# Half of the value weights by a transposing DMA, in a two-layer attention and feed-forward kernel

## The chip, the cores and the metric

The kernel runs on one core of one Trainium2 chip. The time is what the device takes for one execution, in microseconds (us); a run's figure comes from one such execution, and several runs are given by their median. The engines are called PE (TensorE: matmuls; PEld is its loading of weights), DVE (VectorE), ACT (ScalarE), POOL (GpSimd) and SP (SyncE, which here only issues DMAs). Line numbers such as L164 are lines of the kernel; many operations go through a helper, so that they share one line and are told apart by the tiles they read and write.

## The reference, cut to what matters

Four steps, with two functions used twice, on x of 2048 rows and 448 columns:

```
x = x + A(layernorm(x)); x = x + B(layernorm(x)); x = x + A(layernorm(x)); x = x + B(layernorm(x))

A: segments of 32 rows, one after the other, with 8 memory rows ahead of each
   h = concat(mem, segment)
   q, k, v = h @ Wq, h @ Wk, h @ Wv          # 16 heads of 256; each weight is 448 x 16 x 256
   p = softmax(q @ k.T * scale, masked)
   o = sum over heads of (p @ v) @ Wo[head]   # Wo: 16 x 256 x 448
   mem = o[:8]; output = o[8:]
B: h = relu(x @ W_gate) * (x @ W_up); output = h @ W_down     # 448 x 1792, 448 x 1792, 1792 x 448
```

All inputs are bf16.

## The kernel before

The weights of A enter only as products of two of them, so the kernel works these out first, once. For each head it makes `A_sb`, Wq times the transposed Wk (448 x 448 a head), and `B_sb`, Wv times Wo (448 x 448 a head). The main part, which takes most of the time, then runs over the 64 segments of both layers with these products, with the feed-forward blocks in between. The change is in the preparation alone.

The preparation goes by positions of two heads each (512 columns of a weight matrix); there are 8 (`NP`). In its first loop, position p of the query and key weights makes `A_sb`: products named `aps`, `mxw` and `apl`. In its second loop, position p of the value weights makes `B_sb`: products named `bps`, with `wo`, the rows of Wo for these heads. I call the first the query-key stage and the second the value stage; a position of the first is also called a pair, of Wq and Wk.

A product on TensorE sums over the partitions, so the products need each weight with the head's columns on the partitions, while a row of the DRAM tensor holds 4096 columns. So the kernel loads a block as it lies (`load_nat`, L345 on: 384 of 448 rows, as three blocks of 128, into one of six buffers `nat`), and turns it on TensorE by products with an identity (`flip`: six turns into a bank of PSUM called `tpw`, then one copy on DVE or ACT to `qk` or `vT`). The last 64 of the 448 rows are loaded apart, for two blocks at a time into the two halves of the partitions of one of three buffers `natl` (`load_last`), and turned by `flip_last` (four turns into `tpl`, one copy). For the query and key weights the two blocks are Wq and Wk of one position; for the value weights they are two neighbouring positions, and the copy goes to `v3`, which keeps all eight.

`ask(p)` issues the loads of a position, two positions ahead of its use; `queue(p)` and `queue_v(p)` return the tile that a position's products will read, and a list of pieces of work (the flips). The loops take one piece after each product of the position before, so that the flips of position p + 1 stand between the products of position p. Which of DVE and ACT copies a bank is decided when the program is written, by a small plan of how long each is taken (`one_of`); which bank a product takes is decided in the same way (`bank`).

The order of matmuls on TensorE is fixed (`in_order`). The order of the loads on SP is not: a scheduler puts the instructions of an engine in an order by when they could start, so a load that waits for no buffer can move ahead of others that do. A load waits for the buffer's last reader, and also for the DMA eight places before it, because eight completion semaphores are used in turn. `load_wo` issues the loads of `wo` on POOL's queue, each held back until TensorE has come to that place (`spread`); `next_piece` does so on SP for the up weights.

Position 1 of the value stage is followed by the layernorm of the first rows (`normed(row_stats(xp[1]))`: statistics on DVE, a power on POOL, the result `xn` on DVE), and position 2 by their turn on TensorE (`first_rows`).

The main part uses transposing DMAs already: `hk`, `PT` and `xT` are written to DRAM and read back turned, all on SP.

Of the kernel before, what the change touches and what calls it, by code (L numbers as in the profile page):

```python
# [8 lines left out]
BF = mybir.dt.bfloat16  # L9
# [6 lines left out]
DM = 448  # L16
H = 16
NP = 8
# [45 lines left out]
def build_kernel(ctx, tc, A_x, A_mem0, A_Wq, A_Wk, A_Wv, A_Wo, B_W_gate, B_W_up, B_W_down, out,  # L64
                 ntiles=16, nseg=64):
    nc = tc.nc
    P = nc.NUM_PARTITIONS
# [6 lines left out]
    Wv = A_Wv.rearrange("d h e -> d (h e)")  # L74
# [66 lines left out]
    def bank(shape, dtype, name, after=700, hold=False):  # L141

        i = min((i for i in range(8) if i not in held), key=lambda i: free_at[i])
        t = psum.tile(shape, dtype, tag=f"b{i}", name=name)
        bank_of[t.name] = (i, after)
        free_at[i] = now[0] + 1000
        if hold:
            held.add(i)
        return t
# [13 lines left out]
    def mm(out, lhsT, rhs, **k):  # L163
        in_order(nc.tensor.matmul(out, lhsT, rhs, **k))  # L164
        n = 1
        for d in out.shape[1:]:
            n *= d
        pair = lhsT.shape[0] <= 64 or lhsT.shape[-1] == 64 and out.shape[0] == 64
        passed(out, max(25, n / 2.4 + 2.5) * (0.5 if pair else 1))

    def tr(out, src, idn):
        in_order(nc.tensor.transpose(out, src, idn))  # L172
        passed(out, 56)
# [15 lines left out]
    pre = prepare.enter_context(tc.tile_pool(name="pre", bufs=6))  # L189
# [3 lines left out]
    def rows3(src, cols):  # L193
        return src[0:384, cols].rearrange("(k p) n -> p k n", p=P)
# [140 lines left out]
    with prepare:  # L335
# [9 lines left out]
        def load_nat(src, p):  # L345
            t = nats[nn[0] % 6]
            nn[0] += 1
            nc.sync.dma_start(t[:], rows3(src, slice(512 * p, 512 * p + 512)))
            return t

        def load_last(parts):
            t = nats3[n3[0] % 3]
            n3[0] += 1
            for r, (src, p) in zip(FR, parts):
                nc.sync.dma_start(t[r, :], src[384:448, 512 * p:512 * p + 512])
            return t

        asked = {0: (nats[0:2], nats3[0])}

        def ask(p):  # L360

            if p < NP:
                asked[p] = ([load_nat(src, p) for src in (Wq, Wk)], load_last(((Wq, p), (Wk, p))))
            elif p < 2 * NP:
                asked[p] = (load_nat(Wv, p - NP),
                            load_last(((Wv, p - NP), (Wv, p - NP + 1))) if p % 2 == 0 else None)

        def ask_second():

# [7 lines left out]
                    asked[1] = (nats[2:4], load_last(((Wq, 1), (Wk, 1))))  # L377
            nn[0] = 4

        v3 = pre.tile([P, NP, 4, 64], BF, name="v3", bufs=1)  # L380
        until = {dve: 0.0, act: 0.0}

        def one_of(n, per):
# [6 lines left out]
        def share(dst, src, n, per):  # L390
            evac(one_of(n, per), dst, src)

        def flip(nat, e2, dst):
            tp = bank([P, 2, 512], BF, "tpw")
            for kd in range(3):
                for e in range(2):
                    tr(tp[:, e, kd * 128:(kd + 1) * 128],
                       nat[:, kd, (2 * e2 + e) * 128:(2 * e2 + e + 1) * 128], ident[:])
            share(dst, tp[:, :, 0:384], 768, (0.6, 0.82))

        def flip_last(nat, dst):
            tp = bank([P, 4, 128], BF, "tpl")
            for e in range(4):
                tr(tp[:, e, :], nat[:, e * 128:e * 128 + 128], ident[:])
            share(dst, tp[:].rearrange("p e (i d) -> p e i d", i=2), 512, (0.6, 0.82))

        def queue(p):
            if p < NP:
                nat, last = asked[p]
                qk = pre.tile([P, 4, 2, DM], BF, tag="qk", name="qk", bufs=2)  # L410
                us = [lambda i=i, e2=e2: flip(nat[i], e2, qk[:, 2 * e2:2 * e2 + 2, i, 0:384])
                      for e2 in range(2) for i in range(2)]
                us.insert(2, lambda: flip_last(last, qk[:, :, :, 384:DM]))
                return qk, us
            return queue_v(p - NP)

        def queue_v(p):
            us = []
            nat, last = asked[p + NP]
            if p % 2 == 0:  # L420
                us.append(lambda: flip_last(last, v3[:, p:p + 2].rearrange("p a e d -> p e a d")))
            vT = pre.tile([P, 4, 384], BF, tag="vT", name="vT", bufs=2)
            return vT, us + [lambda e2=e2: flip(nat, e2, vT[:, 2 * e2:2 * e2 + 2, :]) for e2 in range(2)]

        def first_rows(xn0):
# [20 lines left out]
        def by_heads(ps, a, b, n):  # L446
            for t in range(2):
                for eo in range(2):
                    mm(ps[FR[eo], 0:n], a(2 * eo + t), b(2 * eo + t), start=(t == 0), stop=(t == 1),
                       tile_position=(0, 64 * eo))  # L450
# [15 lines left out]
        for p in range(NP):  # L466
            hf, p4 = divmod(p, 4)
            qk = ready
            ask(p + 2)
            ready, us = queue(p + 1)  # L470
            todo += us
# [26 lines left out]
        def last_out(p, wo):  # L498

            ps = bank([P, 512], F32, "bps")  # L500
            by_heads(ps, lambda e: v3[:, p, e, :], lambda e: wo[:, e, :], DM)
            hf, p4 = divmod(p, 4)
            share(B_sb[:, hf, 24 + p4, 0:DM], ps[:, 0:DM], DM, (1.28, 0.85))

        for p in range(NP):
            hf, p4 = divmod(p, 4)
            vT = ready
            ask(p + 2 + NP)
            ready, todo = queue_v(p + 1) if p + 1 < NP else (None, [])
            wo = wos.pop(0)  # L510
            if p % 2:
                last_out(p, wo)
            for eo in range(2):
                for kd in range(3):
                    bps = bank([P, 512], F32, "bps")
                    for t in range(2):
                        e = 2 * eo + t
                        mm(bps[:, 0:DM], vT[:, e, kd * 128:(kd + 1) * 128], wo[:, e, :],
                           start=(t == 0), stop=(t == 1))
                    share(B_sb[:, hf, tidx(kd, eo, p4), 0:DM], bps[:, 0:DM], DM, (1.28, 0.85))  # L520
                    if kd < 2 and todo:
                        todo.pop(0)()
            if p % 2 == 0:
                last_out(p, wo)
            if p == 1:
                xn0 = normed(row_stats(xp[1]))
            if p == 2:
                first_rows(xn0)
            if p + 3 < NP:
                load_wo(p + 3)  # L530
            if p >= 3:
                next_piece()
                next_piece()
# [196 lines left out]
    def project_early(hf, chains, hb, j, pairs=(0, 1), head=0, after=700):  # L730

        n = L * len(chains)
        pre = {}
        for pair in [EARLY[i] for i in pairs]:
            for i0 in pair:
                pre[i0] = bank([P, 512], F32, "prj", 700 if i0 else after, hold=True)
            for i in range(head):
                tile_of(pre[pair[0]], hf, pair[0] + i, i, chains, hb, j, range(3), i == 0, False)
            for i in range(6):
                for i0, rows in zip(pair, (slice(0, 64), slice(64, 128))):  # L740
                    mm(pre[i0][:, i * n:(i + 1) * n], A_sb[rows, 3, hf, a_tile(i0 + i), :], moving(hb, j, 3, chains, rows),
                       start=(i == 0 and (head == 0 or i0 != pair[0])), stop=False, skip_group_check=True)
        return pre
# [97 lines left out]
    def active(g):  # L841
        return [c for c in (0, 1) if 0 <= g - c * LAG < nseg]
# [364 lines left out]
    pre, late = project_early(0, active(0), hTb[0], 0), None  # L1207
    for g in range(nsteps):
# [6 lines left out]
        if g % 2 and 0 <= i < nblk + LAG // BLK - 1:  # L1215
            fed = Feed(i)
            pre, late = step(g, fed, pre, late)
        else:
            pre, late = step(g, None, pre, late)
# [27 lines left out]
@with_exitstack  # L1247
def kernel(
    ctx: ExitStack,
    tc: tile.TileContext,  # L1250
    A_x: bass.AP,
    A_mem0: bass.AP,
    A_Wq: bass.AP,
    A_Wk: bass.AP,
    A_Wv: bass.AP,
    A_Wo: bass.AP,
    A_seg_len: bass.AP,
    B_x: bass.AP,
    B_W_gate: bass.AP,
    B_W_up: bass.AP,  # L1260
    B_W_down: bass.AP,
    out: bass.AP,
):
    S = A_x.shape[1]
    ntiles = S // 128
    build_kernel(ctx, tc, A_x, A_mem0, A_Wq, A_Wk, A_Wv, A_Wo, B_W_gate, B_W_up, B_W_down, out,
                 ntiles=ntiles, nseg=4 * ntiles)
# [35 lines left out]
```

## Time and profile before

| | |
|---|---|
| median of 3 runs | 1534.79 us (1534.61 to 1541.23) |
| the profiled execution, its own time | 1534.4 us |
| its span in the profile | 1532.6 us |
| granted TensorE clock | 1.0 |
| query-key stage | to about 42.1 us |
| value stage | 42.1 to 70.7 us |
| main part | from 70.7 us |
| matmuls | 40395 |

The span is the time between the first and last recorded event; the execution's own time is 1.8 us longer. The page of the profile gives the busy time of each engine, the same in 40 slices of 38.3 us, the chain of work that ended last, and groups of instructions. The trace behind it can be asked for stretches of time (busy time of each engine, share of the 16 DMA engines that was busy, and rate), for the instructions of one tile, for an engine's instructions in order, and for how long a DMA took from its issue to its landing. The busy time of TensorE counts matmuls whose ends are modelled; it is not the same as work at full rate.

### The profile page before, as it was taken

The numbers are of one execution on the slowest core, as the hardware profiler recorded it, in microseconds if no ns is written. First come the engines' busy times: TensorE is split into PE (matmuls) and PEld (weight loads), VectorE is DVE, ScalarE is ACT, GpSimd is POOL, SyncE is SP. The second block draws the span as 40 slices with busy tenths as digits, with TensorE's granted clock in tenths as the row PEclk, the third lists the DMA queues.
The fourth block names the chain that finished last, engine by engine and source line by source line (L and its number), as shares of the span: only waits on it lengthen the run. The fifth ranks groups of instructions, "written<-read, shape, count | busy, mean of one in ns | idle before, by whom it ended". The sixth has DMA issues, their size and how long they took to land.

```text
span 1532.6 us, 88890 instructions
## 1 busy us (share of the span) xinstructions
PE 1519.7 (99%) x40395; PEld 1410.9 (92%) x40395; DVE 1079.3 (70%) x3595; ACT 727.9 (47%) x1999; POOL 66.7 (4%) x169
## 2 busy tenths in 40 slices
PE   9999999999999999999999999999999999999998
PEld 6689999999999999999999999999999999999997
DVE  7766777777767677776677777776777777677765
ACT  6744444454444444544444445444444444444444
POOL 3300000000000000000000000000000000000000
PEclk9999999999999999999999999999999999999999
DMA  8620111111111111111111111111111111111100
GB/s 255 204 69 21 31 38 40 30 35 36 34 33 33 40 37 32 36 36 38 31 33 40 37 31 36 36 36 29 37 40 36 31 37 36 32 29 37 30 7 9
DMA packets 148873, 66.96 MB, mean 44 GB/s; under 512 B 108488, under 2 KB 147600, under 8 KB 148496
## 3 DMA queue, kind: packets, MB, share of 16 engines
q1 hardware_dynamic: 114688, 49.22, 12.5%
q10 hardware_dynamic: 32720, 8.38, 2.9%
q8 instruction: 316, 5.18, 1.4%
q0 software_dynamic: 1088, 3.68, 0.7%
q14 instruction: 61, 0.50, 0.1%
HBM read 23.18 MB, written 19.46 MB: 28 GB/s over the span
## 4 chain that ended last, share of the span: by engine, by line
PE 96%; DMA 2%; DVE 2%; issue 0%; POOL 0%; ACT 0%; POOLq 0%; DVEq 0%
PE prj L164 31%; PE ox L164 25%; PE gps L164 6%; PE ups L164 6%; PE dps L164 6%; PE o L164 5%; PE y L164 4%; PE Sx L164 3%; PE bps L164 1%; PE Sm L164 1%; PE ya L164 1%; PE yb L164 1%; PE tpw L172 1%; PE aps L164 1%; DMA xT<-dxn 1%; PE pps L172 1%
## 5 line engine op out<-in xcount | busy, mean ns | idle before, releaser
L164 PE MATMUL prj<-hT,A_sb 128*128 128x80 bf16 (+3 forms) x15232 | 540.3, 199 | 0.4 <-ACT hT L106 0.4
L164 PEld LDWEIGHTS <-A_sb 128*128 128x128 bf16 (+1 forms) x15232 | 500.8, 99 | 20.3 <-issue 0.7
L164 PEld LDWEIGHTS <-B_sb 128*128 128x128 bf16 (+1 forms) x15008 | 484.6, 103 | 15.3 <-issue 2.3
L164 PE MATMUL ox<-Y,B_sb 128*128 128x80 bf16 (+2 forms) x11256 | 436.1, 200 | 2.0 <-issue 2.0
L106 ACT CAST TQ<-prj 128x480 bf16<-128x480 f32 (+1 forms) x380 | 184.8, 498 | 94.8 <-PE prj L164 81.3
L106 ACT CAST Y<-y 128x128 bf16<-128x128 f32 (+2 forms) x452 | 150.3, 411 | 108.3 <-PE y L164 102.6
L106 DVE CAST Y<-y 128x256 bf16<-128x256 f32 (+2 forms) x316 | 135.5, 479 | 39.9 <-PE y L164 39.3
L106 ACT ACTIVATE se<-se 128x160 f32<-128x160 f32 (+2 forms) x270 | 82.0, 304 | 150.2 <-DVE se L106 141.7
L106 DVE CAST TQ<-prj 128x480 bf16<-128x480 f32 (+1 forms) x228 | 125.9, 572 | 8.0 <-PE prj L164 7.6
L164 PE MATMUL gps<-xT,Wg_sb 128*128 128x128 bf16 (+3 forms) x1904 | 128.7, 215 | 0.1
L106 DVE SCALAR_TENSOR_TENSOR hh<-gps,ut 128x512 bf16<-128x512 f32 (+2 forms) x136 | 78.1, 595 | 61.9 <-PE gps L164 39.8
L164 PEld LDWEIGHTS <-Wu_sb 128*128 128x128 bf16 (+1 forms) x1904 | 105.1, 97 | 5.7 <-issue 0.2
L164 PE MATMUL ups<-xT,Wu_sb 128*128 128x128 bf16 (+3 forms) x1632 | 107.0, 216 | 2.6 <-DMA xT<-dxn 2.1
L164 PEld LDWEIGHTS <-Wg_sb 128*128 128x128 bf16 (+1 forms) x1904 | 106.8, 97 | 2.7 <-issue 2.4
L164 PEld LDWEIGHTS <-hk 40*128 40x128 bf16 (+1 forms) x1950 | 99.1, 96 | 8.1 <-issue 0.4
L106 ACT CAST TZ<-prj 64x320 bf16<-64x320 f32 (+2 forms) x264 | 96.8, 377 | 18.8 <-DVE TZ L106 15.9
L106 ACT CAST ut<-ups 128x512 bf16<-128x512 f32 (+1 forms) x102 | 57.5, 564 | 82.1 <-PE ups L164 82.1
L106 ACT COPY os<-o 64x16 f32<-64x16 f32 (+3 forms) x134 | 25.7, 192 | 146.2 <-PE o L164 144.5
L106 DVE TENSOR_REDUCE ssum<-se 128x4 f32<-128x160 f32 (+2 forms) x270 | 73.2, 271 | 30.3 <-ACT se L106 26.5
L164 PE MATMUL dps<-Wd_sb,hh 128*128 128x448 bf16 (+1 forms) x504 | 93.3, 342 | 0.8 <-DVE hh L106 0.8
L106 DVE CAST Y<-ya 128x256 bf16<-128x256 f32 x134 | 56.9, 425 | 47.0 <-PE ya L164 46.5
L164 PEld LDWEIGHTS <-TQ 128*128 128x128 bf16 x1938 | 85.7, 96 | 1.3 <-ACT TQ L106 0.9
(141 smaller groups left out, 1726.2 us busy)
## 6 DMA issues: line engine op xcount, KB each, us to landing
dh<-hT ACTq DMA_DIRECT2D x60, 128.0 KB, 2.2
dx<-PX SPq DMA_DIRECT2D x90, 64.0 KB, 1.6
dxn<-xn SPq DMA_DIRECT2D x29, 128.0 KB, 2.6
wo<-in_A_Wo_dram POOLq DMA_DIRECT2D x8, 448.0 KB, 4.8
nat<-in_A_Wv_dram SPq DMA_DIRECT2D x8, 384.0 KB, 4.4
nat<-in_A_Wq_dram SPq DMA_DIRECT2D x6, 384.0 KB, 4.3
nat<-in_A_Wk_dram SPq DMA_DIRECT2D x6, 384.0 KB, 4.9
xa<-in_A_x_dram SPq DMA_DIRECT2D x32, 56.0 KB, 2.6
```

The source lines that it names most:

```text
L106: r = f(*a, **k)
L164: in_order(nc.tensor.matmul(out, lhsT, rhs, **k))
L172: in_order(nc.tensor.transpose(out, src, idn))
```

## The change

Of the eight value positions, those with an odd number are no longer loaded as they lie and turned on TensorE. One transposing DMA on SP reads all 448 rows of the position's 512 columns and writes them turned, 128 x 4 x 448, into a tile `vTd` with two buffers. The products of such a position read `vTd`, including the last 64 rows, which no longer come from `v3`. Even positions go on as before, but the tail loads of two neighbouring even positions now share a buffer, `v3` holds four positions, and `vT` has one buffer.

```diff
             elif p < 2 * NP:
-                asked[p] = (load_nat(Wv, p - NP),
-                            load_last(((Wv, p - NP), (Wv, p - NP + 1))) if p % 2 == 0 else None)
+                v = p - NP
+                if v % 2:
+                    vT = pre.tile([P, 4, DM], BF, tag="vTd", name="vTd", bufs=2)
+                    nc.sync.dma_start_transpose(vT[:], Wv[:, 512 * v:512 * v + 512])
+                    asked[p] = vT
+                else:
+                    asked[p] = (load_nat(Wv, v), load_last(((Wv, v), (Wv, v + 2))) if v % 4 == 0 else None)
...
-        v3 = pre.tile([P, NP, 4, 64], BF, name="v3", bufs=1)
+        v3 = pre.tile([P, NP // 2, 4, 64], BF, name="v3", bufs=1)
...
         def queue_v(p):
             us = []
+            if p % 2:
+                return asked[p + NP], us
             nat, last = asked[p + NP]
-            if p % 2 == 0:
-                us.append(lambda: flip_last(last, v3[:, p:p + 2].rearrange("p a e d -> p e a d")))
-            vT = pre.tile([P, 4, 384], BF, tag="vT", name="vT", bufs=2)
+            if p % 4 == 0:
+                us.append(lambda: flip_last(last, v3[:, p // 2:p // 2 + 2].rearrange("p a e d -> p e a d")))
+            vT = pre.tile([P, 4, 384], BF, tag="vT", name="vT", bufs=1)
             return vT, us + [lambda e2=e2: flip(nat, e2, vT[:, 2 * e2:2 * e2 + 2, :]) for e2 in range(2)]
...
         def last_out(p, wo):
 
             ps = bank([P, 512], F32, "bps")
-            by_heads(ps, lambda e: v3[:, p, e, :], lambda e: wo[:, e, :], DM)
+            by_heads(ps, lambda e: vT[:, e, 384:DM] if p % 2 else v3[:, p // 2, e, :], lambda e: wo[:, e, :], DM)
```

In the changed program's order of issue on SP, the transposing DMAs of value positions 1 and 3, which wait for no buffer, stand among the loads of the query and key weights: the first right after the row load `xp` that follows pair 2's loads, the second after the tail loads of pair 3 and right before the `nat` loads of pair 3. The load of another row block, which stood in the first one's place, comes later. Those of positions 5 and 7 stand in the value stage: position 5's waits for the last product of position 1, position 7's stands behind the first two pieces of the up weights.

## The prediction, made before the changed kernel was run

> **What bounds the kernel now.** I read the page first, then the chain of work that ended last, restricted to the preparation, then stretches of time, the tiles that the change touches, and the transposing DMAs that the kernel already has.
>
> ```profile
> span 1532.6 us, 88890 instructions
> ...
> PE 1519.7 (99%) x40395; PEld 1410.9 (92%) x40395; DVE 1079.3 (70%) x3595; ACT 727.9 (47%) x1999; POOL 66.7 (4%) x169
> ...
> DMA  8620111111111111111111111111111111111100
> ```
>
> TensorE bounds the whole, and DMA is loaded in the first two slices alone. The change touches the preparation, which ends at 70.7 us, where the first prj products start: 4.6% of the span. So even a large effect there is small in the total; about 0.5% (7.7 us) is what a measurement of this kernel can tell from no change.
>
> ```profile
> 12.60 0.43 PE aps L164 x2
> ...
> 13.51 4.20 DMA nat<-in_A_Wk_dram
> 17.71 0.05 issue
> 17.76 0.51 PE tpw L172 x6
> ...
> 19.26 0.34 PE tpw L172 x6
> ```
>
> This is the chain between 10 and 22 us (start, length, what). The Wk load of pair 3 is issued at 13.51, lands at 17.71, and the flips that read it start at once. That load has no slack. Six flips take 0.34 us.
>
> ```profile
> 222.70:223.50 0.80, 0.80 (x29) 0.69 (x27) 0.16 (x1) 0.56 (x2) 0.00 (x0) 1.00 0.64 144
> 12.00:13.75 1.75, 1.69 (x19) 1.07 (x19) 1.11 (x3) 1.67 (x5) 1.75 (x2) 1.00 0.52 152
> 14.00:32.00 18.00, 17.91 (x230) 13.44 (x228) 15.32 (x34) 13.85 (x33) 0.63 (x2) 1.00 0.92 291
> 42.10:70.80 28.70, 28.40 (x245) 16.35 (x245) 23.39 (x47) 20.65 (x37) 10.83 (x14) 1.00 0.63 205
> ```
>
> Stretches: busy us of PE, PEld, DVE, ACT and POOL, then granted clock, DMA share, GB/s. From 14 to 32 us the DMA engines are 92% busy at 291 GB/s: the query-key stage lives on the edge of its loads. Between 12 and 13.75 us they are 52% busy, so 0.84 us of DMA time is free there. The value stage (42.1 to 70.8 us) is TensorE's: 28.4 of 28.7 us, with DMA at 63%. The first row is one isolated transposing DMA (hk, 448 rows of 256 B, 112 KB): 0.64 x 0.80 = 0.51 us of all 16 engines.
>
> ```profile
> L172 PE MATMUL tpw<-ident,nat x288: 219/219/314, 4.1 to 65.8; 128*128 128x128 bf16 x144
> L106 DVE COPY qk<-tpw x31: 547/558/559, 5.0 to 37.8; 128x768 bf16<-128x768 bf16 x31
> L106 DVE COPY vT<-tpw x11: 547/558/559, 41.0 to 66.2; 128x768 bf16<-128x768 bf16 x11
> L106 ACT COPY vT<-tpw x5: 799/800/800, 48.7 to 65.3; 128x768 bf16<-128x768 bf16 x5
> ```
>
> The flips (288 in all, 96 of them of value weights) and their 16 copies for the value weights.
>
> ```profile
> PT<-dx SPq DMA_TRANSPOSE x90, 2.4
> hk<-dh SPq DMA_TRANSPOSE x60, 3.2
> ...
> xT<-dxn SPq DMA_TRANSPOSE x30, 3.5
> ```
>
> Median us from issue to landing of the three existing transposing DMAs, of 64, 112 and 128 KB. Each holds SP's queue for 1.15 to 1.21 us, without regard to its size. The new one moves 448 KB.
>
> **The change, part by part.**
>
> *Removed flips.* Value positions 1, 3, 5 and 7 lose two groups of six flips each: 8 x 0.34 = 2.72 us. The tail flips for pairs (2,3) and (6,7) go too, those for positions 0 and 2 and for 4 and 6 stay: two groups of four, 0.22 us each by the chain, 0.44 us. All of it lies on TensorE in the value stage: 3.16 us saved at most. Each odd position's last product now reads its tail from the DMA's tile; the products themselves keep their shapes and number.
>
> *Removed copies.* Eight vT copies (mostly 0.56 us on DVE, some 0.80 on ACT) and two tail copies (0.42). Worth nothing of their own: in the value stage DVE works 23.4 and ACT 20.7 of 28.7 us, beside TensorE. After the change an even position (0, 2, 4, 6) has no flips between its products, so a product pair of 0.38 us must be emptied every 0.38 us; DVE (0.62) and ACT (0.53) together empty one in 0.29 us. The cover holds.
>
> *A stall that grows.* After position 1 the first token rows are normalised on DVE, which waits for POOL (behind a wo load of 0.75 us on its queue):
>
> ```profile
> 51.43 0.61 DVE L106 TENSOR_SCALAR xn<-xp,mv,rstd 128x448 bf16<-128x448 bf16 x2 [1.02 <-POOL rstd L106]
> 51.94 1.15 DVE L106 CAST B_sb<-bps 128x448 bf16<-128x448 f32 x2
> ```
>
> DVE empties no bank from 49.6 to 51.9 us. TensorE lost only 0.3 us at that place because position 2 carried 0.68 us of flips for position 3. Those go, so the products reach the filled banks, and the token transposes reach xn, earlier. Bounds: nothing, if eight banks suffice, and 1.4 us, if the 0.68 us of cover and another 0.7 are lost. I take 0.6 (nearest to the 0.68).
>
> *Moved loads, value stage.* The four removed nat loads and two pairs of tail loads leave the queue at 29 to 44 us, where the wo loads of 38.9 us took 6.2 us to land (45.1), just when position 1 wanted them (45.2). With less traffic they should take the 3.7 to 4.9 us that later wo loads take; position 1 starts 0.7 us sooner and is still served. Worth 0. The transposing DMA of position 5 waits for the last product of position 1 to free its buffer; it issues some 6 us into the stage, behind it on SP stands a row load and the up weights, which nobody reads before 123 us, and its reader comes some 15 us into the stage. That of position 7 stands behind two up-weight pieces, three or more us early. Both 0; if each came late by its whole service, 2.05 us as worked out below, it would be 4.1, which the range holds.
>
> *The transposing DMAs that move ahead.* This is the part that costs. Those of positions 1 and 3 need no buffer to come free, and in the changed program's order of issue they stand on SP ahead of pair 3's loads: the first in place of an x load that was issued at 10.10 us (which moves behind pair 5's loads and is not read for 100 us), the second right before pair 3's Wq load. Every SP load waits for the landing of the load eight places before it: that Wq load issued at 12.47, when pair 2's Wq (7.35 + 5.1) had landed. Now the first transposing DMA holds SP from 10.1 to 11.3, two tail loads follow to 12.5, the second transposing DMA holds it to 13.7, and pair 3's Wq and Wk issue at about 13.8 and 14.3, 1.3 and 0.8 us later than before. But the bytes decide, not the issue: 2 x 448 KB now stand ahead of pair 3.
>
> Service of one: by the isolated hk, 0.51 us for 448 packets of 256 B; the new one has 1792 such packets, so 4 x 0.51 = 2.05 us, 4.1 us for two. Off go the x load (56 KB, 0.2 us at 291 GB/s) and the 0.84 us that DMA had free. Pair 3 lands 4.1 - 0.2 - 0.8 = 3.1 us later, and TensorE, which waits for it with no slack, loses 3.0. Lower bound: at 291 GB/s a block takes 1.58 us, delay 2.1. Upper bound: the slope of the landing times, (3.5 - 2.4) us for 64 KB more, gives 7.7 us for 448 KB, delay 2 x 7.7 - 1.0 = 14.4. I take 3.0, since the service row is of the same packets, without the waiting that the medians include. If SP were held in proportion to bytes (4.2 us instead of 1.2), the Wq load would issue near 19.8 and the delay would be about 6.5; the equal 1.15 to 1.21 us for 64 to 128 KB speak against it.
>
> After pair 3, everything on TensorE is 3 us later, and so are the loads behind it; pair 5's issue by landings that move less, so no second stall follows.
>
> [...]
>
> *Sum.* -3.16 + 0.6 + 3.0 = +0.4 us. The profiled execution took 1534.4 us (span 1532.6 and 1.8 around it): 1534.8. The median of the three runs is 0.4 above that execution, so 1535.2.
>
> **The rivals.**
>
> 1. *The transposing DMAs cost nothing.* They fill free DMA time, pair 3 is hardly late, and the flips are saved: 3.16 less a stall of 0.6, so 1534.8 - 2.6 = 1532.2; without the stall 1531.6. For it: the free 0.84 us. Against: loads without slack, DMA at 92% after it. Chance 0.2.
> 2. *Big transposing DMAs are slower per byte than small ones,* because 1792 packets of 256 B are fetched from rows 8 KB apart (the rows of hk's source follow on each other) or SP is held. Service 3 to 5 us each: delay 5 to 9, total +2.4 to +6.4, 1537.2 to 1541.2. Chance 0.18.
> 3. *A transposing DMA works block by block at a fixed pace: slower.* PT has 2 blocks of 128x128, hk 3.5, xT 4, and their medians 2.4, 3.2 and 3.5 lie on a line of 0.55 us a block; 14 blocks then take 7.7 us. With service T each, the total is 2T - 1.0 - 2.6 us, negative below 1.8 us, and past +7.7 from T = 5.7 us. At 7.7 it is +11.8: 1546.6. For it: that line. Against: the isolated hk, whose packets were through in 0.8 us. [...] Chance 0.1.
>
> A gain over 0.5% would need 7.7 us where 3.16 are removed; I leave 0.01 for it.
>
> **How the numbers follow.** The likeliest, near cancellation: 1535.2, chance 0.51, own range 1533.5 to 1537. The range must take in rival 1 (1531.6) and rival 2 (1541.2): 1531.6 to 1541.2. Beyond it lie rival 3 and little else. Slower by over 0.5%: rival 3 and a corner of rival 2, 0.11. Faster 0.01, the rest 0.88.
>
> **What would show it.** In the changed profile TensorE should wait for nat of pair 3 near 17 us, about 3 us in one or two waits, with the value stage 2.5 us shorter, and the prj products starting within 1 us of 70.7. 56 fewer matmuls. vTd landings alone near 4 us, near 6 in the crowd. DVE's wait for rstd should stay and a wait of bps or tps behind it grow to near 1 us. The forecast is wrong if pair 3 is not waited for, if the vTd landings are above 8 us, or if any wait for vTd itself shows.

## The result, and the profile after

The changed kernel takes 1543.35 us (median of 22 runs, 1535.35 to 1552.89); 22 runs of the kernel before, beside them, 1537.97. The ratio is 1.0033, 95% interval [1.0022, 1.0043]: 5.1 us slower, 3.4 to 6.6. The runs beside it lie 3.2 us above the three that the prediction started from; on their level the ratio gives 1539.9. The forecast was 1535.2, with a range of 1531.6 to 1541.2: the measured median lies above the range, and the difference to the kernel before, +5.1 instead of +0.4, is what has to be explained.

Three lines of the page of the changed kernel: span, busy engines, and the DMA share in slices of 38.6 us.

```profile
span 1542.9 us, 88747 instructions
...
PE 1520.3 (99%) x40339; PEld 1409.8 (91%) x40339; DVE 1076.1 (70%) x3589; ACT 722.9 (47%) x1995; POOL 66.4 (4%) x169
...
DMA  8630111111111211111111111111111111111100
```

56 matmuls are gone, as forecast. The span is 10.3 us longer than before's, but only half of that is the change: prj starts at 75.53 us instead of 70.68 (+4.85), and the main part, whose code the change leaves alone, took 1467.4 us instead of 1461.9. Further down the main part of one and the same program is seen to differ by 8 us from one execution to the next, and the profiled execution of before, 1534.4 us, was shorter than all 22 of its runs. So the +4.85 is what the profiles say of the change, and the ratio agrees with it.

The chain of work that ended last, from 16.6 us on (start, length, what):

```profile
16.63 5.26 DMA nat<-in_A_Wq_dram
21.89 0.05 issue
21.93 0.82 PE tpw L172 x6
22.76 0.64 PE aps L164 x2
23.40 0.11 PE mxw L164 x2
23.50 0.64 PE tpw L172 x6
```

TensorE does wait for pair 3's `nat`, as forecast, but for its Wq load, and longer. And when the load is there, the first six flips take 0.82 us, two products 0.64 and the next six flips 0.64, where before two products took 0.33 and six flips 0.34 (0.51 right behind a wait): TensorE runs at about half its rate.

SP's queue (start, how long the instruction held SP, what), after, and the same place before:

```profile
9.81 3.80 SPq L368 DMA_TRANSPOSE vTd<-in_A_Wv_dram  x1
...
14.93 1.60 SPq L368 DMA_TRANSPOSE vTd<-in_A_Wv_dram  x1
16.63 0.53 SPq L348 DMA_DIRECT2D nat<-in_A_Wq_dram  x1
17.26 0.42 SPq L348 DMA_DIRECT2D nat<-in_A_Wk_dram  x1
```

```profile
12.47 0.55 SPq L348 DMA_DIRECT2D nat<-in_A_Wq_dram  x1
13.51 0.37 SPq L348 DMA_DIRECT2D nat<-in_A_Wk_dram  x1
```

The first transposing DMA held SP for 3.80 us and the second for 1.60, where 1.2 each was assumed, and pair 3's Wq was issued at 16.63 us, not at 13.8.

Stretches of the changed kernel (busy us of PE, PEld, DVE, ACT, POOL, granted clock, DMA share, GB/s):

```profile
12.00:14.00 2.00, 1.91 (x24) 1.29 (x23) 1.34 (x4) 1.87 (x6) 2.00 (x3) 1.00 1.31 119
14.00:15.00 1.00, 1.00 (x16) 0.74 (x13) 0.95 (x4) 0.76 (x2) 0.61 (x2) 1.00 1.27 289
15.00:17.00 2.00, 1.99 (x27) 1.47 (x25) 1.86 (x5) 1.39 (x5) 0.00 (x0) 1.00 0.52 130
17.00:20.00 3.00, 0.00 (x0) 0.00 (x0) 0.28 (x1) 0.44 (x2) 0.00 (x0) 1.00 1.05 255
20.00:27.00 7.00, 5.07 (x36) 3.86 (x37) 1.80 (x4) 1.43 (x3) 0.00 (x0) 0.52 0.97 289
49.50:75.50 26.00, 25.43 (x179) 13.08 (x177) 20.56 (x40) 17.45 (x33) 10.82 (x14) 1.00 0.73 207
```

Four things are to be seen. Between 12 and 17 us, in which SP is held by the two transposing DMAs until 13.61 and from 14.93 to 16.53, the DMA engines move 119 to 130 GB/s in four of five microseconds; before they moved 163 from 12 to 14 us, when they were 56% busy, and about 290 from 14 us on. (The share adds up the times of packets, and it reads 1.31 and 1.27 here, so they overlap.) TensorE idles from 17 to 21.9 us. From 20 to 27 us its granted clock is 0.52; it was 1.00 in every stretch shown of before. In shorter stretches the half clock can be placed: it lasts from 20.34 to 27.16 us. And the value stage, from 49.50 us to the prj start at 75.53, takes 26.0 us where it took 28.55: the saving of 2.5 us is there.

The waits of TensorE between 10 and 80 us (total, times, longest), and DVE's at the first layernorm:

```profile
PE tpw L172 <- DMA nat<-in_A_Wq_dram: 4.9, 1, 4.9
PE bps L164 <- DMA wo<-in_A_Wo_dram: 0.3, 1, 0.3
```

```profile
58.31 0.61 DVE L106 TENSOR_SCALAR xn<-xp,mv,rstd 128x448 bf16<-128x448 bf16 x2 [1.01 <-POOL rstd L106]
```

No product waits for `vTd` in this execution. So the balance at the prj start is: the value stage starts 7.4 us late (49.50 against 42.13) and is 2.5 us shorter, +4.85.

### The profile page after: what moved, and what is told of

The parts are those of the page before. It is cut to its first block, busy times and chain, and to the rows that moved or that the text cites. A ratio compares the mean times of both kernels' runs of the same rounds, so it can differ in the third digit from the quotient of the medians.

```text
span 1542.9 us, 88747 instructions
## 1 busy us (share of the span) xinstructions
PE 1520.3 (99%) x40339; PEld 1409.8 (91%) x40339; DVE 1076.1 (70%) x3589; ACT 722.9 (47%) x1995; POOL 66.4 (4%) x169
## 4 chain that ended last, share of the span: by engine, by line
PE 94%; DMA 3%; DVE 2%; issue 1%; POOL 0%; ACT 0%; POOLq 0%; DVEq 0%
PE prj L164 30%; PE ox L164 25%; PE gps L164 6%; PE ups L164 6%; PE dps L164 6%; PE o L164 5%; PE y L164 4%; PE Sx L164 3%; PE Sm L164 1%; PE aps L164 1%; PE ya L164 1%; PE yb L164 1%; PE tpw L172 1%; PE pps L172 1%; DMA xT<-dxn 1%
## 5 line engine op out<-in xcount | busy, mean ns | idle before, releaser
L106 DVE CAST Y<-y 128x256 bf16<-128x256 f32 (+2 forms) x316 | 135.5, 479 | 43.1 <-PE y L164 42.5
L106 ACT CAST ut<-ups 128x512 bf16<-128x512 f32 (+1 forms) x102 | 57.4, 563 | 83.2 <-PE ups L164 83.2
L164 PE MATMUL y<-PT,hk 40*128 40x256 bf16 (+1 forms) x1280 | 86.4, 249 | 3.0 <-DMA PT<-dx 3.0
```

Source lines behind the costliest of these rows:

```text
L106: r = f(*a, **k)
```

## The experiments

Theory L (late loads; the expectations call it S, and later hold or placement): the two transposing DMAs ahead of pair 3's loads make TensorE wait, the wait makes its clock fall, and the rest of the change brings the 2.5 us that were forecast. Rival B (bytes): it is the 2 x 448 KB, whatever kind of DMA brings them. Rival M: something in the main part got slower. Rival C (cover): flips that are taken out of the value stage come back there as waits. The prj start of each profile is set against 70.68 and 71.64 us, which two profiles of the kernel before gave.

### Both kernels once more

No edit: the kernel before, and then the changed one.

> The kernel before, unchanged, run as an experiment, so that its profile is from the same chip as the next three. All theories: prj products start near 70.7 us, ratio to itself 1.000 within 0.1%. What it is for: the length of the main part (span less the start of the prj products, 1461.9 us in the first profile of before, 1467 to 1472 in those of the changed kernel and its variants). If the main part is 1466 us or more here, the difference between those profiles is chance between executions and chips; if it stays near 1462, rival M (the main part became slower) lives.

Measured: value stage from 43.1, prj at 71.64 us, main part 1462.0; ratio 0.9999 [0.9987, 1.0011]. The preparation of the same program can differ by 1 us. By what was set down, 1462 leaves rival M alive. But this profile, too, is of a short execution, the shortest of its 12 (1535.42 us, median 1539.90): if its preparation is typical, the median less 1.8 and 71.64 us leaves 1466.5 for the main part, nearly as long as the changed kernel's.

> The changed kernel, unchanged. Theory S: a wait of about 5 us for pair 3's Wq near 17 us, granted clock 0.5 for some 6 us after it, prj products start between 74.5 and 76 us, 1.002 to 1.004 of the kernel before on this chip; main part as long as that of the kernel before within the chance between executions (some 3 us). Rival M: the main part is 3 us or more longer, or the ratio is above what the prj start explains by 3 us.

Measured: value stage from 48.4, prj at 74.96, a wait of 3.2 us for pair 3 (about 5 was expected), clock 0.50 from 20 to 26 us; ratio 1.0033 [1.0015, 1.0052]. Against the kernel before on the same chip the value stage starts 5.3 us late and prj 3.3 us late; the value stage took 26.6 us. In all ten of its runs the mean clock was 0.997 to 0.999, which is 1.5 to 4.6 us of a span at full clock. It was below 1.0 in 21 of the 22 runs of the result, too, but in only 6 of 30 runs of the kernel before beside these: the fall belongs to the changed kernel, not to one profile.

### The two early DMAs added to the kernel before

All flips stay; the two DMAs stand in the changed kernel's place and write to space that nobody reads before the up weights come.

```diff
+                if v in (1, 3):
+                    nc.sync.dma_start_transpose(Wu_sb[:, :, 224 * v - 224:224 * v + 224], Wv[:, 512 * v:512 * v + 512])
```

> The kernel before with all its flips, plus the two early transposing DMAs of positions 1 and 3 in the same place ahead of pair 3; they write into the space of the up weights, which are loaded over it later, and nobody reads them. It does one part of the change alone. Theory S: the query-key stage ends 5 to 7.5 us later than in the kernel before (at 47 to 49.6 us), the clock falls to 0.5, the value stage keeps its 28.6 us, prj products start at 75.5 to 78.2 us, 1.003 to 1.005 of before. Rival (the loss of the changed kernel comes from its other parts): prj products start within 2 us of 70.7.

Its waits of TensorE:

```profile
PE tpw L172 <- DMA nat<-in_A_Wq_dram: 4.5, 1, 4.5
```

Value stage from 49.0, prj at 77.52: +6.8 us on 70.68 and +5.9 on 71.64, which is of the same chip; the value stage is 28.6 us long as before. Ratio 1.0041 [1.0025, 1.0056], and a mean clock of 0.998 in all five runs. The two DMAs alone make the loss, and 77.5 less the 2.5 us of flips is about the changed kernel. Its main part, whose code is that of before, took 1467.8 us, as the changed kernel's 1467.4: a main part of that length comes without the change's other parts, and rival M has nothing left to explain.

### The wait filled, so that the clock stays

24 products with no use stand where TensorE waits.

```diff
+                    if p == 2 and eo == kd == 0:
+                        keep_warm(24)
```

> The changed kernel, with 24 idle products (5.2 us on a tile of zeros) put on TensorE where it waits for pair 3's Wq. Theory S with the clock as a part of its own: the wait disappears into the products, pair 3's flips start near 21.9 us as before, but at full clock; granted clock 1.0, and the prj products start 2.3 to 2.7 us sooner than in the changed kernel, near 73.1 us; the median 2 to 3 us below the changed kernel's. Rival (the clock falls for another reason, or the slow stretch after the wait is late loads and not the clock): prj products start at 75 us or later.

```profile
20.00:27.00 7.00, 7.00 (x65) 4.41 (x63) 2.33 (x5) 1.91 (x4) 0.00 (x0) 1.00 0.97 289
```

The stretch shows clock 1.00. From the first flip of pair 3 to the prj start it took 50.74 us (23.37 to 74.11), against 53.60 in the changed kernel (21.93 to 75.53): 2.9 us are the clock's. Pair 3 itself came 1.4 us later here (a tail load held SP for 1.35 us, and Wq was issued at 17.55), so prj started at 74.11, where 73.1 was expected; ratio 1.0014 [0.9997, 1.0031] against 1.0033. The mean clock was 1.0 in nine of its ten runs, and in none of the ten runs of the changed kernel above: the filled wait keeps the clock up, not in the profile alone.

### The same bytes by plain DMAs, and one transposing DMA instead of two

```diff
-                    nc.sync.dma_start_transpose(vT[:], Wv[:, 512 * v:512 * v + 512])
+                    if v < 4:
+                        flat = vT[:].rearrange("p e d -> p (e d)")
+                        nc.sync.dma_start(flat[:, 0:1536].rearrange("p (k n) -> p k n", k=3),
+                                          rows3(Wv, slice(512 * v, 512 * v + 512)))
+                        nc.sync.dma_start(flat[:, 1536:1792], Wv[0:128, 512 * v:512 * v + 256])
+                    else:
+                        nc.sync.dma_start_transpose(vT[:], Wv[:, 512 * v:512 * v + 512])
```

> The changed kernel, but positions 1 and 3 fetch their 448 KB by plain DMAs (384 and 64 KB) in the place of the transposing ones; the turn of these two positions is left out, so their products are of the unturned weights. Theory S1 (a transposing DMA costs more than its bytes: it holds SP for 1.5 to 3.8 us and leaves the DMA engines partly idle): the wait for pair 3 falls from 5.1 us to 1.5 to 2.5 us, no halved clock, prj products start at 69.5 to 71 us. Theory S2 (the bytes ahead are the cost): the wait stays at 4 us or more and the clock falls.

```profile
PE tpw L172 <- DMA nat<-in_A_Wq_dram: 1.0, 1, 1.0
PE tpw L172 <- DMA nat<-in_A_Wk_dram: 0.8, 1, 0.8
```

SP's queue there:

```profile
13.43 0.43 SPq L370 DMA_DIRECT2D vTd<-in_A_Wv_dram  x1
13.96 0.43 SPq L348 DMA_DIRECT2D nat<-in_A_Wq_dram  x1
...
17.35 0.48 SPq L372 DMA_DIRECT2D vTd<-in_A_Wv_dram  x1
```

Value stage from 44.4 (+2.3), prj at 69.87. Each plain DMA held SP for 0.43 to 0.48 us, one for 1.32, and Wq was issued at 13.96; the last 64 KB went behind pair 3's loads. So in this profile the bytes cost 2.3 of the 7.4 us in this place (rival B), and the other 5 come from their being transposed. The runs do not settle that split. The ratio was 1.0021 [1.0002, 1.004], where this profile's gain of 0.8 us would lie below 1, and its interval overlaps with that of the changed kernel; the mean clock was 0.996 to 0.999 in seven of its ten runs and 1.0 in the one that was profiled. In most executions the clock fell somewhere even here.

```diff
+                    r = nc.sync.dma_start_transpose(vT[:], Wv[:, 512 * v:512 * v + 512])
+                    if v == 3:
+                        spread(r)
```

> Only the transposing DMA of position 1 stands ahead of pair 3; that of position 3 is held back until the value stage. Theory S (each of the two costs its hold of SP and its service): a wait for pair 3 of 1.5 to 3 us, no halved clock or a short one, prj products start at 69.5 to 71.5 us. If the first alone makes the loss (its 3.8 us hold): wait of 4 us or more with the clock halved, prj products at 74 us or later.

```profile
PE tpw L172 <- DMA nat<-in_A_Wq_dram: 2.8, 1, 2.8
```

SP held for 3.47 us by the one that is left; value stage from 45.5 (+3.4), prj at 71.55, ratio 1.0017 [1.0002, 1.0032]. In this profile the first DMA makes about half of the loss. It makes nearly all of the late issue: Wq was issued at 16.22 us, 0.4 sooner than in the changed kernel, but landed 3.8 us after that instead of 5.26. The second one then costs by what it adds to that landing, and by the clock, which stayed up here after a wait of 2.78 us:

```profile
20.00:27.00 7.00, 6.74 (x85) 5.03 (x86) 5.04 (x11) 4.71 (x12) 0.00 (x0) 1.00 0.99 297
```

That is not the rule for this kernel either: its mean clock was below 1.0 in eight of ten runs.

### Pair 3's loads on another queue

The transposing DMAs stay; the two `nat` loads of pair 3 are issued by ACT.

```diff
-            nc.sync.dma_start(t[:], rows3(src, slice(512 * p, 512 * p + 512)))
+            (nc.scalar if p == 3 and src is not Wv else nc.sync).dma_start(t[:], rows3(src, slice(512 * p, 512 * p + 512)))
```

> The changed kernel with one difference: the nat loads of pair 3's Wq and Wk are issued from ACT's queue instead of SP's, so they no longer stand behind the transposing DMAs on SP, while the bytes that compete for the DMA engines are the same. Theory hold (most of the wait for pair 3 is that SP is held while the DMA engines go partly idle): the wait of TensorE for pair 3's nat falls from 5 us to between 1 and 2.5 us, the clock does not fall, the prj products start at 70 to 72 us; ratio 1.000 to 1.001. Theory service (the bytes of the transposing DMAs take that long on the DMA engines): the wait stays at 4 us or more, the clock falls as in the changed kernel, prj at 74 to 76 us; ratio 1.003.

TensorE's queue of that kernel, a stretch, and the landings of the two loads:

```profile
13.22 1.04 PE L172 MATMUL tpw<-ident,nat 128*128 128x128 bf16 x12 [2.49 <-ACT A_sb L106]
```

```profile
14.00:17.00 3.00, 3.00 (x20) 1.37 (x18) 1.90 (x4) 2.38 (x7) 0.63 (x2) 0.50 0.98 291
```

```profile
DMA to landing us min/median/max: 4.3/5.4/6.5
```

The wait for pair 3's loads fell from 5 us to 0.4. They were issued at 12.25 and 12.82 us and landed 4.3 and 6.5 us later; the Wk load landed at 19.3 us where before's landed at 17.7. In the changed kernel it landed at 22.9 (17.26 + 5.6). So beside two transposing DMAs (which held SP for 2.35 and 3.20 us) the load comes 1.6 us late (although it was issued 0.7 us sooner than before), behind them on their queue 5.2. The order on the queue is most of it. The wait itself proves less, since TensorE came to pair 3 later here. A new wait took its place: ACT waited for the landing of an earlier load before it could issue these (it copied nothing for 4.43 us), its copies stood behind, TensorE idled 2.49 us, and the clock fell again. prj at 72.24 us, just above the 70 to 72 of the held queue; ratio 1.0018 [1.0006, 1.003], above its 1.000 to 1.001; both fit that new wait and the clock, but no run took them away.

### All four held back

Each transposing DMA is held until TensorE has come to a place; position 1's from pair 6 on (near 34 us), the others two positions ahead of their use.

```diff
+                    vT = pre.tile([P, 4, DM], BF, tag="vTd", name="vTd", bufs=2)
+                    spread(nc.sync.dma_start_transpose(vT[:], Wv[:, 512 * v + 512:512 * v + 1024]))
+                    asked[p + 1] = vT
```

> All four transposing DMAs are held back on SP until TensorE has come to a given place (position 1's until the end of pair 5, position 3's until the value stage begins), so that none stands ahead of pair 3's loads; the flips stay dropped. Theory S (the loss is the wait for pair 3 behind the two early transposing DMAs, 5 us, plus about 2.5 us of halved TensorE clock after it): no wait for nat near 17 us, granted clock 1.0 throughout, prj products start near 68.2 us (70.7 less the 2.5 us that the value stage saved in the changed kernel), median 2 to 3 us below the kernel before. Rival M (something in the main part, its banks or queues, is slower with the new tiles): prj products start early too, but the median stays 2 us or more above the kernel before. Rival V (the transposing DMAs crowd the value stage): vTd or wo is waited for there and prj products start after 70.7 us.

```profile
PE bps L164 <- DVE mv L106: 1.4, 1, 1.4
PE bps L164 <- DMA wo<-in_A_Wo_dram: 0.6, 1, 0.6
```

The query-key stage is that of before (value stage from 42.3, no wait for pair 3), but prj started at 69.99, not at 68.2: the value stage took 27.7 us. Ratio 1.0004 [0.999, 1.0018]. Next, positions 1 and 3 both from 34 us on:

```diff
+                for u in (1, 3) if v == 0 else (v + 2,) if v in (3, 5) else ():
+                    vT = pre.tile([P, 4, DM], BF, tag="vTd", name="vTd", bufs=2)
+                    spread(nc.sync.dma_start_transpose(vT[:], Wv[:, 512 * u:512 * u + 512]))
+                    asked[u + NP] = vT
```

> All four transposing DMAs held back, but those of positions 1 and 3 both issued near 34 us, when the flips of the last pairs begin and the DMA engines were idle in the kernel before; those of positions 5 and 7 after the last reader of their buffer. Theory S: no wait for pair 3, value stage begins near 42.2 us, no wait for wo of position 2 behind a transposing DMA (in the earlier variant it took 7.2 us to land and position 2 began 1.4 us late), prj products start at 68.0 to 69.0 us; median 1 to 3 us below the kernel before, if the clock does not fall at the start of the main part. Rival: the saved flips come back as another wait in the value stage, prj products at 69.5 us or later, median equal to before.

```profile
PE bps L164 <- DMA wo<-in_A_Wo_dram: 1.3, 2, 0.7
PE bps L164 <- DVE B_sb L106: 0.7, 1, 0.7
PE bps L164 <- DVE A_sb L106: 0.7, 1, 0.7
```

```profile
34.28 8.48 SPq L370 DMA_TRANSPOSE vTd<-in_A_Wv_dram  x2
49.83 1.48 SPq L370 DMA_TRANSPOSE vTd<-in_A_Wv_dram  x1
```

prj at 70.68, where 68 to 69 was expected; value stage 28.0 us; ratio 1.0012 [0.9997, 1.0028]. The two in the crowd held SP for 8.48 us in all, the later one, on an idle queue, 1.48. Most of the saved flips came back as waits for `wo` and for banks: rival C holds here. In the changed kernel it does not (value stage 26.0 us): there the same two had landed by 19 us, long before the first `wo` was issued, at 41.95.

### Two of the four, in two places

Positions 3 and 7 alone, one buffer, position 3's issued from pair 6 on (the tail loads are paired anew, and the others are flipped):

```diff
-                if v % 2:
+                if v in (0, 4):
+                    vT = pre.tile([P, 4, DM], BF, tag="vTd", name="vTd", bufs=1)
+                    spread(nc.sync.dma_start_transpose(vT[:], Wv[:, 512 * v + 1536:512 * v + 2048]))
+                    asked[p + 3] = vT
```

> Only value positions 3 and 7 come by transposing DMA, each held back until TensorE has come to a place where nothing urgent stands behind it on SP (position 3's at the start of pair 6's loads, near 34 us; position 7's after the last reader of position 3's). The other six positions are flipped as before. It saves four groups of six flips (4 x 0.34 = 1.36 us) and one tail group (0.22 us), 1.58 us. Theory hold (the loss of the change is SP held ahead of pair 3 and the clock that follows, and where nothing urgent stands behind a transposing DMA it costs nothing): no wait for pair 3 above 2.5 us, clock 1.0, the value stage starts at 42 to 43 us, the prj products at 69.1 to 69.8 us; ratio to the kernel before 0.998 to 1.000. Theory cover (flips taken out of the value stage come back as waits for wo and for banks, as when all four were held): the value stage stays at 28 to 28.7 us, the prj products start at 70.5 or later; ratio 1.000 to 1.002.

```profile
37.00:43.00 6.00, 5.74 (x71) 4.02 (x69) 5.23 (x13) 4.80 (x12) 0.77 (x1) 1.00 1.31 97
43.00:47.00 4.00, 0.20 (x2) 0.14 (x3) 0.39 (x1) 0.20 (x1) 0.75 (x1) 1.00 0.97 238
47.00:50.00 3.00, 3.00 (x18) 2.02 (x17) 0.93 (x2) 1.06 (x2) 0.00 (x0) 0.50 1.05 374
```

In this execution, one of the two longest of its 12, position 3's DMA, issued at 34.75 us, held SP for 3.70 us, and from 37 to 43 us all transfers together moved 97 GB/s, though the DMA engines' records show them busy (share 1.31). `wo` landed 11.7 us after its issue, TensorE waited 4.1 us for it, and the clock fell to 0.50. prj at 77.7. The ratio of all runs, 1.0009 [0.9993, 1.0025], and a clock of 1.0 in nine of 12 say that this is not the rule. The same kernel, profiled once more:

> The same program as the one with positions 3 and 7 alone, a second look at its profile. In the first look, one of the two longest of its 12 executions, wo of the first value position landed 11.7 us after its issue, behind position 3's transposing DMA, at about 100 GB/s for 8 us. If a transposing DMA in a crowd always does that, the wait for wo of 4 us and the clock fall after it return here, and prj starts near 77.7. If it is a matter of chance, as the clock of 1.0 in ten of those 12 executions suggests, the wait for wo is under 1.5 us, SP is still held for 3 us or more (the queue is full), and prj starts at 69 to 71 us.

```profile
39.00:41.00 2.00, 2.00 (x27) 1.28 (x21) 1.72 (x5) 1.87 (x6) 0.77 (x1) 1.00 1.23 113
41.00:43.00 2.00, 2.00 (x25) 1.43 (x24) 1.97 (x6) 1.53 (x4) 0.00 (x0) 1.00 1.20 339
```

Here the slow stretch lasted 2 us; SP was held 2.53 us (forecast 3 or more), the wait for `wo` was 0.8, prj at 70.6. So with a transposing DMA among plain ones all transfers together fell to 113 GB/s for 2 us in one profile, and to 97 for 6 in the other; the kernel before moved 329 GB/s from 37 to 41 us.

Then positions 5 and 7 alone, which are issued in the value stage itself, at 49.7 and 59.5 us, where SP has nothing urgent behind them:

```diff
+                if v in (4, 6):
+                    vTd = pre.tile([P, 4, 2, DM], BF, tag="qk", name="vTd", bufs=2)
+                    vT = vTd[:, 0:2].rearrange("p a b c -> p (a b) c")
+                    spread(nc.sync.dma_start_transpose(vT, Wv[:, 512 * v + 512:512 * v + 1024]))
+                    asked[p + 1] = vT
```

> Only value positions 5 and 7 come by transposing DMA, both issued inside the value stage (near 50 to 61 us), when SP has only row and up-weight loads behind them and the DMA queue has little in it; the other six are flipped as before, and the query-key stage is that of the kernel before. It saves 28 products, four groups of six flips (4 x 0.34 us) and one tail group (0.22 us), 1.58 us of TensorE work. Theory placement (the saving is real wherever the transposing DMA meets a queue with little in it; the loss of the change comes from the two that are issued into the loads of the query-key stage): SP is held 1.5 to 1.7 us by each, landings 5 to 7 us, no wait for wo above 0.5 us, clock 1.0, the value stage takes 27.0 to 27.3 us instead of 28.6, prj starts at 69.1 to 69.4 us (70.0 to 70.3 where the kernel before gives 71.6); ratio 0.998 to 1.000. Theory cover (flips taken out come back as waits for wo and banks wherever they are taken out): the value stage stays above 28 us, prj at 70.5 or later; ratio 1.000 to 1.001.

```profile
PE bps L164 <- DMA vTd<-in_A_Wv_dram: 0.9, 1, 0.9
PE bps L164 <- DVE B_sb L106: 0.3, 1, 0.3
```

Ratio 0.9987 [0.9977, 0.9997], the only interval that lies below 1. But in the profile prj started at 70.51: the value stage took 28.1 us, since position 7's DMA landed 8.0 us after its issue and its reader waited for it (0.9 us of idle products; 1.3 us by the loading of weights). So position 7's was issued one position sooner, and the same kernel was run once more beside it (the columns that the DMA reads change with it):

```diff
-                if v in (4, 6):
+                if v in (4, 5):
```

> As the kernel with positions 5 and 7 alone, but position 7's transposing DMA is issued one position sooner (near 53 us instead of 59.5), since there it landed 8.0 us after its issue and TensorE waited 1.3 us for it. Theory placement: no wait for vTd, the value stage takes 27.0 to 27.3 us, prj starts at 69.1 to 69.6 us (70.0 to 70.5 where the kernel before gives 71.6); ratio 0.998 to 0.9995, a little under the 0.9987 of the version before it. Theory cover: the 1.3 us come back as a wait for wo (which shares the DMA engines with it from 53 us) or for banks, prj at 70.5 or later; ratio as before it or above, 0.9985 to 1.000.

> The kernel with positions 5 and 7 alone once more, on another set of runs. Theory placement: the ratio lies below 1 again (0.998 to 0.9995), the wait for vTd of about 1 us returns, prj at 70.3 to 71. Theory chance: the 0.9987 of its first 12 runs was chance, and the ratio is 0.9995 to 1.0005.

One sooner (54.8 us): no wait for `vTd`, but 0.5 us for `wo` and more for banks; the value stage took 28.1 us (43.21 to 71.29), ratio 0.9995 [0.9981, 1.001]; the 27.0 to 27.3 us that were expected did not come. The repetition: ratio 0.9991 [0.9974, 1.0007], prj at 69.17 us, and no wait for `vTd` this time.

```profile
42.20:69.20 27.00, 26.70 (x209) 14.65 (x209) 21.88 (x43) 19.03 (x35) 10.81 (x14) 1.00 0.77 223
```

In this profile the value stage took 27.0 us instead of 28.55: the 1.55 us that two positions' flips cost (forecast 1.58). The two ratios, 2.0 and 1.4 us below before, agree with that, though the second interval holds 1, and the first profile showed a gain of 0.45 us only. This is the one version that seems to beat the kernel before, by 0.1%; the runs do not show it beyond doubt. The main parts of the two executions of this one program, 1466.3 and 1474.2 us, are the 8 us of chance spoken of at the start.

## Why the prediction was wrong

The forecast was 1535.2 us, +0.4 on before; measured are +5.1, which is what its second rival (SP held, or large transposing DMAs slower) gave as +2.4 to +6.4, with a chance of 0.18. That its number fits is partly luck: it reached it by a service of 3 to 5 us each, and the clock had no place in it. A change within 0.5% had 0.88, and that is what came.

| step of the prediction | forecast | measured |
|---|---|---|
| flips removed, less the stall at the layernorm | -2.56 | -2.5 (value stage 28.55 to 26.0) |
| wait of a product for rstd and banks | near 1 us | none above 0.3 us; 0.5 for the turn of `xn` |
| service of one transposing DMA | 2.05 us | 1.6 us of data for position 5, alone, at about 290 GB/s |
| SP held by each of the two early ones | 1.15 to 1.21 us | 3.80 and 1.60 |
| pair 3's Wq issued at | 13.8 us | 16.63 |
| wait for pair 3 | 3.0 us | 4.9 |
| TensorE's clock | not spoken of, so nothing | half for 6.8 us, 2.5 to 2.9 us lost |
| sum at the prj start | +0.4 | +4.85 |

*The step that failed* is "The transposing DMAs that move ahead": its term, +3.0, measured +7.4 (a wait of 4.9 and 2.5 at half clock). Two parts of it were wrong.

First, "the bytes decide, not the issue". The bytes came out smaller than assumed (1.6 us of data for the one that could be seen alone), and plain DMAs of the same bytes cost 2.3 us in their profile. The issue decided: the first DMA held SP for 3.1 to 4.2 us in five profiles that leave the order on SP as it is (3.80, 3.87, 3.47, 3.06, 4.18), always until 13.5 to 14.1 us, and in the changed kernel the data moved at 119 to 130 GB/s around it, less than half of 291. The 1.15 to 1.21 us are medians of DMAs of 64 to 128 KB in the main part, where the DMA engines are mostly 10 to 20% busy, while this one is 448 KB and stands behind loads. Even there 36 of the 180 held SP for more than 1.3 us, up to 2.35: the medians hid that the hold varies. The prediction had the case in hand (SP held in proportion to bytes, Wq at 19.8, delay 6.5) and put it aside by a row of another situation.

Second, the sum stopped at the wait. A wait of that length costs more than itself here: TensorE's clock fell at 20.34 us, about 3.4 us after TensorE had become idle, and came back at 27.16, 5.2 us after the work had resumed; half of 5.2 is 2.6 us. Filling the wait with useless products gave 2.9 us back. In the repeat of the changed kernel and in the kernel with the two DMAs added the clock fell 2.3 and 2.1 us after TensorE had become idle, so even the forecast wait of 3.0 us should have been priced with the clock, as a risk.

*What held.* The place of the loss, the saving, the worthlessness of the copies, and the value stage's own two DMAs, for which no product waited. The fit of the saving is partly luck: in the value stage TensorE had some 2.8 us less work, not 3.16, and idled 0.3 us more, not 0.6. The third rival (a fixed pace by blocks, 7.7 us each) is refuted by the changed kernel's landings of 4.0 to 6.6 us for all 14 blocks. They stood the other way round than forecast: 6.6 us alone, 6.0 and 4.0 in the crowd.

*What stays open.* That the hold grows with what stands in the queue is read from where it was long (behind other loads, 1.9 to 4.2 us) and short (an idle queue, 1.48 to 1.59); no run varied the queue alone, and what SP waits for meanwhile is not seen. The second early DMA, some 5 us behind the first, held SP for only 1.60 to 1.70 us, so standing among loads is not enough. What decides whether the slow stretch at about 100 GB/s lasts 2 or 6 us isn't known, nor why the clock fell in most runs of the plain version and not in its profile.

## What to carry to other kernels

Before a DMA is moved ahead on a queue, ask how long its issue holds that queue behind the loads that are already there, not only how many bytes it brings: a transposing DMA of 448 KB held SP for 3 to 4 us in front of loads without slack, and 1.5 us on an idle queue. Price a stall of TensorE with its clock, as a risk: here 5 us of waiting cost 7.4, in two other profiles the clock fell 2.3 and 2.1 us into the same wait, and a wait of 2.78 us cost only itself in the one profile of it. Work taken off the bounding engine is a gain only where the next waits (`wo`, banks) have slack: of all the later placements, only two DMAs at a quiet place, each soon before its use, gave their 1.5 us, and that in one of two profiles.

## What the runs showed of the hardware that was not expected

The half clock came in two lengths. Seven of the 16 profiled executions have a mean clock of 0.997 to 0.999, the others 1.0. In six of the seven, stretches before the end show the half clock: it lasted about 6.8 us (the changed kernel twice, the two DMAs added, all four held) or about 3.4 us (loads on ACT, the first profile with positions 3 and 7). In the seventh (position 7 one sooner, 0.999) no stretch shows it. So the price is not in proportion to the wait: idle times of 4.9, 3.2, 4.5 and 1.53 us belong to the longer ones, 2.49 and 4.1 to the shorter. In the changed kernel 1.6 of the 6.8 us lay in the wait itself, and 5.2 in work.

The clock also fell after shorter idleness than the 3.4 us of the changed kernel's profile. In the kernel with the loads on ACT it fell after TensorE had idled 2.49 us, and in the kernel with all four held it fell at the start of the main part, after 1.53 us in which TensorE had no work:

```profile
80.00:88.00 8.00, 7.77 (x218) 7.34 (x219) 3.55 (x15) 2.33 (x7) 0.00 (x0) 0.57 0.13 34
```

The length of a wait does not decide it: one of 2.78 us left the clock up. What does is open.

In the changed kernel the first data of the transposing DMA of position 5, on an idle queue, moved about 1.5 us after its issue (issued at 55.92, data from 57.4 us at about 290 GB/s, landed 6.6 us after issue): 1.6 of 6.6 us are data.
